# Float64 weights to float32 by bit shifts in a fused attention, mixture-of-experts and dense kernel

## Chip, cores and metric

The kernel runs on one core of one Trainium2 chip. The metric is the device time of one execution in microseconds. [...]

## The reference

```python
# attention, per head; q, k, v: (4, 12, 448, 64) float32
scores = cap * np.tanh(scale * np.matmul(q, k.transpose(0, 1, 3, 2)) / cap)
attn = softmax(scores); x = attn @ v            # -> (1792, 768)
# experts: 8 experts of 4 slots; w1 (8, 768, 1024), w2 (8, 1024, 768) float32
logits = x @ phi                                 # (1792, 32)
slot_input = softmax(logits, axis=0).T @ x
slot_out = relu(slot_input[e] @ w1[e]) @ w2[e]   # for each expert e
x = softmax(logits, axis=1) @ slot_out
# dense layer: w_in (768, 2048), w_out (2048, 768)
r = np.maximum(x @ w_in, 0.0)
return (s * (r * r) + b) @ w_out                 # (1792, 768) float32
```

The cap is 30. w_in and w_out reach the kernel as float64 (their scale factor is a double), 12.6 MB each; all other inputs are float32.

## The kernel before

The kernel writes its instruction order by hand: a planner (`ListSchedule`) gets each piece of work with an engine, a cost, its needs and its buffers, simulates the engines with these costs, and emits the pieces in the order in which they would start. Each engine then works through its own queue in that order and waits where a semaphore asks for it. There is one plan for attention and one for the dense layer; the stage between them is in plain program order.

Attention walks over 24 pairs of heads. TensorE makes scores (`sp`, L452), ScalarE takes tanh and exp (L459, L472), GpSimd sums exponentials over rows (`es`, L482 and L485), TensorE multiplies with v (`av`, L494), and VectorE copies and splits q, k and results (L355, L402, L578). For matmuls in the fast float32 format operands are split into a high and a low part.

w_in and w_out are cut into 32 tiles of 128 x 768 weights (even numbers from w_in, odd from w_out). `load_words` reads a tile of float64 as pairs of 32-bit words, low word first, 768 KB. The converter works in three functions: `conv_a` masks out the exponent as 16-bit numbers (`ce`, L206) and the top 20 bits of the mantissa with a leading one set (`cm`, L207) on VectorE; `conv_f` (L214) rebuilds the exponent on ScalarE; `conv_b` puts the sign in (L217) and adds the low word (L221) on VectorE; `conv_m` (L227) multiplies mantissa by power of two on GpSimd. The first 14 tiles are converted within attention (pieces `cl`, `ca`, `cf`, `cb`, `cmul`, `cst` of the first plan) and stored as float32 in DRAM (`scr`), to be loaded again later; when the last is stored, `cend` frees room and opens the further loads of expert weights. The other 18 tiles are converted inside the dense layer (`ld`, `ca`, `cf`, `cb`, `w`).

Between the two lie the slots and the experts: weights of 48.6 MB stream in through rings of buffers (`w1c`, `w2c`), the later ones in room that attention gives back.

The dense layer goes in 64 steps: four blocks of tokens (three of 512, one of 256) times 16 column groups f. A step makes h by one matmul (`gp`, L1091), squares and scales it on ScalarE (L1108, L1115, L1121 twice), takes the low part on VectorE (`gl`, L1136), and adds to the result by matmuls of L1159 and L1160 with the high and low parts of h and of w_out. For each f of the first block the weights must be ready: w_out is split into high (L1046, L1048) and low (L1051, GpSimd); w_in is multiplied with the slot outputs (`ma`, `ms`, `mb`, `mc`, `ml`, L1060 to L1084). Output leaves in L1168 to L1179.

At the very end a flag decides whether everything runs once more in a safe form (`run(True)`); before, the flag depends on the cap alone and the second run does not happen on these inputs.

Of the kernel before, what the change touches and what calls it, by code (L numbers as in the profile page):

```python
# [1 line left out]

# [6 lines left out]
F32 = mybir.dt.float32  # L9
F32R = mybir.dt.float32r  # L10
I32 = mybir.dt.int32
# [8 lines left out]

CAP_FAST = 32.0
EPS = 1e-9


ACT, DVE, POOL, PE, SP = "ACT", "DVE", "POOL", "PE", "SP"
# [66 lines left out]
def kernel(  # L92
# [54 lines left out]
    capsq = const.tile([1, 1], F32, name="capsq")  # L147
    nc.vector.tensor_tensor(out=capsq, in0=capt[0:1], in1=capt[0:1], op=ALU.mult)
    nc.vector.tensor_scalar(out=flag, in0=capsq, scalar1=CAP_FAST * CAP_FAST, scalar2=None, op0=ALU.is_gt)


    wide = w_in.dtype != F32
# [37 lines left out]
    def load_words(i, pool):  # L190
        kb, fn = (KDM, FC) if i % 2 == 0 else (1, DM)
        t = pool.tile([128, kb, fn * 2], I32, tag="w", name="w64")
        nc.sync.dma_start(out=t, in_=w_rows(i, 2))
        return t

    def conv_a(t, pool, bufs):
        nn = t.shape[1] * t.shape[2] // 2  # L200
        hi = t.rearrange("p k (f x) -> p (k f) x", x=2)[:, :, 1]
        top = t.rearrange("p k f -> p (k f)").bitcast(U16)
        top = top.rearrange("p (f x) -> p f x", x=4)[:, :, 3]
        e = pool.tile([128, nn], U16, tag="ce", name="ce", bufs=bufs[0])
        m = pool.tile([128, nn], I32, tag="cm", name="cm", bufs=bufs[1])
        nc.vector.tensor_scalar(out=e, in0=top, scalar1=0x7FF0, scalar2=None, op0=ALU.bitwise_and)  # L206
        nc.vector.tensor_scalar(  # L207
            out=m, in0=hi, scalar1=0x000FFFFF, scalar2=0x00100000,
            op0=ALU.bitwise_and, op1=ALU.bitwise_or,
        )  # L210
        return t, top, e, m

    def conv_f(t, top, e, m):
        nc.scalar.activation(out=e, in_=e, func=AF.Relu, scale=8.0, bias=ebias)  # L214

    def conv_b(t, top, e, m):
        nc.vector.scalar_tensor_tensor(  # L217
            out=e, in0=top, scalar=0x8000, in1=e, op0=ALU.bitwise_and, op1=ALU.bitwise_or
        )
        lo = t.rearrange("p k (f x) -> p (k f) x", x=2)[:, :, 0].bitcast(U32)  # L220
        nc.vector.scalar_tensor_tensor(  # L221
            out=m.bitcast(F32), in0=lo, scalar=2.0 ** -32, in1=m, op0=ALU.mult, op1=ALU.add
        )

    def conv_m(t, top, e, m):
        f = m.bitcast(F32)
        nc.gpsimd.tensor_tensor(out=f, in0=f, in1=e.bitcast(BF16), op=ALU.mult)  # L227
        return f


    def run(safe):
# [40 lines left out]
        def cv_f(i, _):  # L272
            conv_f(*env[i])

        def cv_b(i, _):
            conv_b(*env[i])

        def cv_m(i, _):
            env[i] = conv_m(*env[i])

        def cv_store(i, _):
            nc.sync.dma_start(out=scr[i], in_=env.pop(i))
# [399 lines left out]
        def op(name, engs, f, need=(), prio=0.0, acq=(), rel=(), **kw):  # L682
            sch.add(name, engs, lambda e: f(*name[1:], e), need, prio, acq, rel, **kw)
# [133 lines left out]
        for i in range(len(cvs)):  # L817
            pr = CV0 + CVP * i
            op(("cl", i), [(SP, 2.19)], cv_load, [], pr - 6, [("w", i)], lat=LAT, after=CVA)
            op(("ca", i), [(DVE, 0.94)], cv_a, [("cl", i)], pr, [("cm", i), ("ce", i)])  # L820
            op(("cf", i), [(ACT, 0.83)], cv_f, [("ca", i)], pr)
            op(("cb", i), [(DVE, 1.74)], cv_b, [("cf", i)], pr, [], [("w", i)])
            op(("cmul", i), [(POOL, 1.6)], cv_m, [("cb", i)], pr, [], [("ce", i)])
            op(("cst", i), [(SP, 1.1)], cv_store, [("cmul", i)], pr, [], [("cm", i)], lat=LAT)
            need = [("cst", j) for j in range(i + 1)]

# [181 lines left out]
        def gtile():  # L1008
            return ps_g.tile([128, 512], F32, tag="g", name="gp")
# [3 lines left out]
        raw, cva, wih, mst, msb, woh, wol, hg = {}, {}, {}, {}, {}, {}, {}, {}  # L1013

        def is_words(i):
            return wide and i >= 2 * XS

        def load_w(i, _):
            if is_words(i):
                raw[i] = load_words(i, st_p)  # L1020
                return
            raw[i] = cv_p.tile([128, NE1], F32, tag="cm", name="w32")
            if wide:
                nc.sync.dma_start(out=raw[i], in_=scr[i])
            else:
                nc.sync.dma_start(
                    out=raw[i].rearrange("p (k f) -> p k f", k=KDM if i % 2 == 0 else 1), in_=w_rows(i, 1)
                )

        def emit_ca(i, _):  # L1030
            cva[i] = conv_a(raw.pop(i), cv_p, (NCE, NCM))

        def emit_cf(i, _):
            conv_f(*cva[i])

        def emit_cb(i, _):
            conv_b(*cva[i])

        def emit_cm(i, _):
            raw[i] = conv_m(*cva.pop(i))  # L1040

        def emit_hi(f, e):
            t = wo_tile(f)
# [149 lines left out]
        def call(f, *a):  # L1193
            return lambda e: f(*a, e)

        sch.add("sot", [(DVE, 0.3)], call(emit_sot), after=3.2)
        for i in range(NI):
            f, rows = divmod(i, 2)
            pr = float(f)
            if is_words(i):  # L1200
                sch.add(("ld", i), [(SP, 2.19)], call(load_w, i), prio=pr - WL, acq=[("stg", i)], lat=2.0)
                sch.add(
                    ("ca", i), [(DVE, 0.94)], call(emit_ca, i), [("ld", i)], pr, [("cm", i), ("ce", i)]
                )
                sch.add(("cf", i), [(ACT, 0.83)], call(emit_cf, i), [("ca", i)], pr)
                sch.add(("cb", i), [(DVE, 1.74)], call(emit_cb, i), [("cf", i)], pr, rel=[("stg", i)])
                sch.add(("w", i), [(POOL, 1.6)], call(emit_cm, i), [("cb", i)], pr, rel=[("ce", i)])
            else:
                sch.add(("w", i), [(SP, 1.1)], call(load_w, i), prio=pr, acq=[("cm", i)], lat=2.0)
            if rows:  # L1210
                need = [("w", i)] + (["sot"] if f >= WE else [])
                sch.add(("hi", f), [(ACT, 0.73)] + [(DVE, 0.87)] * (f < FD), call(emit_hi, f), need, pr)
                sch.add(("lo", f), [(POOL, 1.76)], call(emit_lo, f), [("hi", f)], pr, rel=[("cm", i)])
            else:
                pm = pr - PM

                d = 0.45 if f > 2 else 0.9
                ga, gb = ("g", ("a", f)), ("g", ("b", f))
                sch.add(
                    ("ma", f), [(PE, d)], call(emit_ma, f), [("w", i), "sot"], pm, [ga], [("cm", i)]  # L1220
                )
                sch.add(("ms", f), [(ACT, 0.16)], call(emit_ms, f), [("ma", f)], pm, [("ms", f)], [ga])
                sch.add(("mb", f), [(PE, d / 2)], call(emit_mb, f), [("ms", f)], pm, [gb], [("ms", f)])
                sch.add(("mc", f), [(ACT, 0.16)], call(emit_mc, f), [("mb", f)], pm)
                sch.add(("ml", f), [(DVE, 0.2)], call(emit_ml, f), [("mc", f)], pm, rel=[gb])
        prev = ["sot"]
        for x, (t0, n, f) in enumerate(steps):
            ph = x - PH
# [67 lines left out]
```

## Time and profile before

| | us |
|---|---|
| median of 3 runs | 684.87 |
| lowest and highest run | 681.32, 689.25 |
| the profiled execution | 681.37 |
| its span, first to last instruction | 679.6 |
| VectorE busy | 423.9 (62%) |
| TensorE busy | 597.6 (88%) |
| ScalarE busy | 411.0 (60%) |
| GpSimd busy | 275.2 (40%) |

PE is TensorE's matmuls, PEld its weight loads, DVE VectorE, ACT ScalarE, POOL GpSimd, SP the queue that issues most DMAs. A busy share counts an instruction from its start to its end, also where it waits inside. A row by stage gives the stretch, its length, then busy us (with the number of instructions) of PE, PEld, DVE, ACT and POOL, then TensorE's granted clock as a share of full speed, the DMA share and GB/s. The stages by the timeline: attention up to 291 us, slots and experts up to 368.8, the dense layer after that, with its last matmul at 671.9.

### The profile page before, as it was taken

How to read it: one execution, taken by the hardware profiler on the slowest of the kernel's cores; microseconds unless marked ns; L12 is line 12 of the kernel's file. 1: busy time of each engine (PE TensorE's matmuls, PEld its weight loads, DVE VectorE, ACT ScalarE, POOL GpSimd, SP SyncE). 2: the span in 40 equal slices, each digit the busy share in tenths (PEclk: the TensorE clock that was granted, in tenths of full speed). 3: DMA queues.
4: the chain of work that ended last, by engine and by line, in shares of the span. 5: the costliest groups of instructions: out<-in, count | busy, mean ns of one | idle time of the engine just before them, and what ended most of it. 6: DMA issues, size and time to landing. Idle time of an engine off the chain costs nothing.

```text
span 679.6 us, 10379 instructions
## 1 busy us (share of the span) xinstructions
PE 597.6 (88%) x3992; PEld 410.8 (60%) x3992; DVE 423.9 (62%) x614; ACT 411.0 (60%) x572; POOL 275.2 (40%) x200
## 2 busy tenths in 40 slices
PE   6987979988898899889866968777999999999995
PEld 4554544554454445446524756555888888888884
DVE  5799998999999996455402799999411112111211
ACT  6978675767697587400004766546666667666693
POOL 1797579769778795200004455565300000000000
PEclk9999898989999999969967988878999999999999
DMA  6798878997658379889999734440020002000201
GB/s 168 199 297 260 255 221 265 291 249 203 178 165 225 104 222 304 324 327 404 406 417 400 253 117 136 145 158 26 18 76 1 1 1 93 1 1 1 93 1 51
DMA packets 58362, 119.94 MB, mean 176 GB/s; under 512 B 4864, under 2 KB 35072, under 8 KB 58304
## 3 DMA queue, kind: packets, MB, share of 16 engines
q1 hardware_dynamic: 57360, 119.09, 53.9%
q8 instruction: 33, 0.54, 0.3%
q10 hardware_dynamic: 944, 0.10, 0.1%
q14 instruction: 25, 0.20, 0.1%
HBM read 97.62 MB, written 11.01 MB: 160 GB/s over the span
## 4 chain that ended last, share of the span: by engine, by line
PE 49%; DVE 34%; DMA 9%; issue 5%; ACT 2%; POOL 1%; SPq 0%; DVEq 0%; ACTq 0%
PE y L1159 19%; PE y L1160 10%; DVE cm L221 5%; DMA w2c<-in_moe_w_dram 5%; DVE cm L207 5%; PE sp L452 4%; PE av L494 4%; DVE ce L206 3%; DVE ks L402 3%; DVE qs L402 3%; DVE ce L217 3%; DVE ks L355 2%; DVE qs L355 2%; PE h1p L915 2%; PE gp L1091 2%
## 5 line engine op out<-in xcount | busy, mean ns | idle before, releaser
L1136 DVE TENSOR_TENSOR gl<-r,gh 128x512 fp32r<-128x512 f32 (+1 forms) x65 | 47.4, 730 | 146.6 <-ACT r L1121 146.3
L1159 PE MATMUL y<-wo,gh 128*128 128x512 f32 x336 | 130.6, 410 | 0.0
L459 ACT ACTIVATE e<-sp,tsc 112x896 f32<-112x896 f32 x96 | 92.6, 1005 | 38.8 <-PE sp L452 32.4
L485 POOL TENSOR_TENSOR es<-es,e 112x448 f32<-112x448 f32 x92 | 111.0, 1217 | 6.6 <-ACT e L472 3.0
L1160 PE MATMUL y<-wo,gh 128*128 128x256 f32 x336 | 96.9, 289 | 0.0
L452 PE MATMUL sp<-qs,ks 128*112 128x448 f32 x384 | 95.6, 390 | 1.5 <-ACT e L459 1.4
L472 ACT ACTIVATE e<-e,capt 112x896 f32<-112x896 f32 x96 | 95.2, 1042 | 0.3
L494 PE MATMUL av<-e,vn 112*64 112x448 f32 x384 | 86.0, 569 | 4.1 <-ACT ce L214 3.1
L452 PEld LDWEIGHTS sp<-qs,ks 128*112 128x112 f32 x384 | 65.5, 182 | 32.4 <-ACT e L459 8.5
L482 POOL TENSOR_TENSOR es<-e 112x448 f32<-112x448 f32 x48 | 66.7, 1404 | 42.2 <-PE dn L513 35.3
L227 POOL TENSOR_TENSOR cm<-cm,ce 128x768 f32<-128x768 f32 x32 | 59.2, 1850 | 51.2 <-DVE cm L221 36.4
L1159 PEld LDWEIGHTS y<-wo,gh 128*128 128x128 f32 x336 | 65.6, 195 | 13.7 <-issue 2.0
L1108 ACT ACTIVATE r<-gp 128x512 f32<-128x512 f32 (+1 forms) x65 | 34.9, 538 | 58.2 <-PE gp L1091 56.9
L1159 PE MATMUL y<-wo,gl 128*128 128x512 f32 x168 | 68.1, 405 | 1.6 <-DVE gl L1136 1.6
L1160 PEld LDWEIGHTS y<-wo,gh 128*128 128x128 f32 x336 | 66.1, 197 | 1.7
L1121 ACT ACTIVATE gh<-r,bt,st 128x512 fp32r<-128x512 f32 (+1 forms) x65 | 49.1, 756 | 1.7
L1121 ACT ACTIVATE r<-r,bt,st 128x512 f32<-128x512 f32 (+1 forms) x65 | 49.1, 756 | 1.6
L494 PEld LDWEIGHTS av<-e,vn 112*64 112x64 f32 x384 | 24.7, 140 | 40.3 <-issue 30.6
L1160 PE MATMUL y<-wo,gl 128*128 128x256 f32 x168 | 48.5, 289 | 0.0
L214 ACT ACTIVATE ce<-ce,ebias 128x768 uint16<-128x768 uint16 x32 | 29.7, 935 | 29.8 <-DVE ce L206 29.8
L221 DVE SCALAR_TENSOR_TENSOR cm<-w,cm 128x768 f32<-128x768 uint32 x32 | 47.2, 1475 | 0.0
L1159 PE MATMUL y<-woe,gh 128*128 128x512 f32 x112 | 44.3, 416 | 0.0
(143 smaller groups left out, 983.6 us busy)
## 6 DMA issues: line engine op xcount, KB each, us to landing
w1c<-in_moe_w_dram SPq DMA_DIRECT2D x24, 1024.0 KB, 9.0
w2c<-in_moe_w_dram SPq DMA_DIRECT2D x26, 768.0 KB, 13.7
w<-in_moe_w_in_dram SPq DMA_DIRECT2D x16, 768.0 KB, 5.3
w<-in_moe_w_out_dram SPq DMA_DIRECT2D x16, 768.0 KB, 4.6
qs<-qs SPq DMA_DIRECT2D x23, 448.0 KB, 4.7
qn<-in_q_dram SPq DMA_DIRECT2D x24, 224.0 KB, 4.1
kn<-in_k_dram SPq DMA_DIRECT2D x24, 224.0 KB, 4.5
vn<-in_v_dram SPq DMA_DIRECT2D x24, 224.0 KB, 5.0
```

What stands on the lines that cost most here:

```text
L221: nc.vector.scalar_tensor_tensor(out=m.bitcast(F32), in0=lo, scalar=2.0 ** -32, in1=m, op0=ALU.mult, op1=ALU.add)
L227: nc.gpsimd.tensor_tensor(out=f, in0=f, in1=e.bitcast(BF16), op=ALU.mult)
L452: nc.tensor.matmul(out=sp[:, cc, 0:S], lhsT=ks[n][:, h, r * P:(r + 1) * P], rhs=qs[n][:, h, i, :], start=(i == 0), stop=(i == 1),)
L459: nc.scalar.activation(out=e, in_=spt.pop((u, h))[:, :, 0:S], func=AF.Tanh, scale=tsc[0:P])
L472: nc.scalar.activation(out=e, in_=e, func=AF.Exp, scale=capt[0:P])
L482: eng.tensor_tensor(out=t, in0=x[:, 0], in1=x[:, 1], op=ALU.add)
L485: eng.tensor_tensor(out=t, in0=t, in1=x[:, cc], op=ALU.add)
L494: nc.tensor.matmul(out=avt[n][64 * h:64 * h + 64, 0:S], lhsT=vt[n][:, h, r, :], rhs=et[u, h][:, cc], start=(r == 0), stop=(r == R - 1),)
L1121: nc.scalar.activation(out=out, in_=in_, func=AF.Identity, scale=st, bias=bt)
L1136: eng.tensor_tensor(out=gl, in0=t, in1=f32(gh), op=ALU.subtract)
L1159: nc.tensor.matmul(out=ya, lhsT=lhsT, rhs=w[:, 0:512], start=first, stop=last)
L1160: nc.tensor.matmul(out=yb, lhsT=lhsT, rhs=w[:, 512:768], start=False, stop=last and i0 == per - 1)
```

## The change

A float32 pattern is now built in integers: the high word shifted left by three and masked, with sign and top exponent bit put back (two VectorE instructions, `conv_a`), plus the low word times 2^-29 (made by ScalarE in `conv_f`), added as an integer (`conv_m`): by GpSimd in attention, by VectorE in the dense layer. This holds only for weights in float32's normal range, so from step 15 of the dense layer on all 32 tiles are loaded a second time and their least and greatest high word is taken (`note_range`); the closing test (`flag_range`) sets the flag of the safe run. The old converter stays under the names `any_a`, `any_f` and `any_m` for that run, which now converts all tiles anew. Costs and buffer releases in the two plans change with it. Since the first two functions no longer share a buffer in one direction, `conv_f` needs the load only; the plans still put it behind `conv_a`.

The diff, without the imports and unchanged surroundings:

```diff
     capsq = const.tile([1, 1], F32, name="capsq")
     nc.vector.tensor_tensor(out=capsq, in0=capt[0:1], in1=capt[0:1], op=ALU.mult)
     nc.vector.tensor_scalar(out=flag, in0=capsq, scalar1=CAP_FAST * CAP_FAST, scalar2=None, op0=ALU.is_gt)
+    big_cap = const.tile([1, 1], F32, name="big_cap")
+    nc.vector.tensor_copy(out=big_cap, in_=flag)
+    onec = const.tile([128, 1], F32, name="onec")
+    nc.vector.memset(onec, 1.0)
...
     def conv_a(t, pool, bufs):
+        nn = t.shape[1] * t.shape[2] // 2
+        hi = t.rearrange("p k (f x) -> p (k f) x", x=2)[:, :, 1]
+        c = pool.tile([128, nn], I32, tag="ce", name="ce", bufs=bufs[0])
+        m = pool.tile([128, nn], I32, tag="cm", name="cm", bufs=bufs[1])
+        nc.vector.tensor_scalar(
+            out=m, in0=hi, scalar1=3, scalar2=0x3FFFFFF8, op0=ALU.logical_shift_left, op1=ALU.bitwise_and
+        )
+        nc.vector.scalar_tensor_tensor(
+            out=m, in0=hi, scalar=-0x40000000, in1=m, op0=ALU.bitwise_and, op1=ALU.bitwise_or
+        )
+        return t, c, m
+
+    def conv_f(t, c, m):
+        lo = t.rearrange("p k (f x) -> p (k f) x", x=2)[:, :, 0].bitcast(U32)
+        nc.scalar.activation(out=c, in_=lo, func=AF.Copy, scale=2.0 ** -29)
+
+    def conv_m(t, c, m, e):
+        (nc.gpsimd if e == POOL else nc.vector).tensor_tensor(out=m, in0=m, in1=c, op=ALU.add)
+        return m.bitcast(F32)
+
+
+
+
+    def any_a(t, pool, bufs):
         nn = t.shape[1] * t.shape[2] // 2
         hi = t.rearrange("p k (f x) -> p (k f) x", x=2)[:, :, 1]
...
-    def conv_f(t, top, e, m):
+    def any_f(t, top, e, m):
         nc.scalar.activation(out=e, in_=e, func=AF.Relu, scale=8.0, bias=ebias)
 
-    def conv_b(t, top, e, m):
+    def any_m(t, top, e, m):
         nc.vector.scalar_tensor_tensor(
             out=e, in0=top, scalar=0x8000, in1=e, op0=ALU.bitwise_and, op1=ALU.bitwise_or
...
-
-    def conv_m(t, top, e, m):
         f = m.bitcast(F32)
         nc.gpsimd.tensor_tensor(out=f, in0=f, in1=e.bitcast(BF16), op=ALU.mult)
         return f
+
+
+    rng = const.tile([128, 2, NI], F32, name="rng")
+
+    def note_range(i, t):
+        hi = t.rearrange("p k (f x) -> p (k f) x", x=2)[:, :, 1].bitcast(F32)
+        for j, o in enumerate((ALU.min, ALU.max)):
+            nc.vector.tensor_reduce(
+                out=rng[:, j, i:i + 1], in_=hi, axis=AX.X, op=o, apply_absolute_value=True
+            )
+
+    def flag_range(ps):
+
+        ends = const.tile([128, 2], F32, name="ends")
+        off = const.tile([128, 2], F32, name="off")
+        for j, (o, lim, out_of) in enumerate(((ALU.min, LEAST, ALU.is_lt), (ALU.max, MOST, ALU.is_ge))):
+            nc.vector.tensor_reduce(out=ends[:, j:j + 1], in_=rng[:, j, :], axis=AX.X, op=o)
+            nc.vector.tensor_scalar(out=off[:, j:j + 1], in0=ends[:, j:j + 1], scalar1=lim, scalar2=None, op0=out_of)
+        nc.tensor.matmul(out=ps[0:1, 0:2], lhsT=onec, rhs=off, start=True, stop=True)
+        tot = const.tile([1, 1], F32, name="tot")
+        nc.vector.tensor_reduce(out=tot, in_=ps[0:1, 0:2], axis=AX.X, op=ALU.add)
+        nc.vector.tensor_tensor(out=tot, in0=tot, in1=big_cap, op=ALU.add)
+        nc.vector.tensor_scalar(out=flag, in0=tot, scalar1=0.0, scalar2=None, op0=ALU.is_gt)
 
 
...
-        def cv_b(i, _):
-            conv_b(*env[i])
-
-        def cv_m(i, _):
-            env[i] = conv_m(*env[i])
+        def cv_m(i, e):
+            env[i] = conv_m(*env[i], e)
...
             op(("cl", i), [(SP, 2.19)], cv_load, [], pr - 6, [("w", i)], lat=LAT, after=CVA)
-            op(("ca", i), [(DVE, 0.94)], cv_a, [("cl", i)], pr, [("cm", i), ("ce", i)])
-            op(("cf", i), [(ACT, 0.83)], cv_f, [("ca", i)], pr)
-            op(("cb", i), [(DVE, 1.74)], cv_b, [("cf", i)], pr, [], [("w", i)])
-            op(("cmul", i), [(POOL, 1.6)], cv_m, [("cb", i)], pr, [], [("ce", i)])
+            op(("ca", i), [(DVE, 1.6)], cv_a, [("cl", i)], pr, [("cm", i), ("ce", i)], [("w", i)])
+            op(("cf", i), [(ACT, 0.83)], cv_f, [("ca", i)], pr, [], [("w", i)])
+            op(("cmul", i), [(POOL, 1.75)], cv_m, [("cf", i)], pr, [], [("ce", i)])
             op(("cst", i), [(SP, 1.1)], cv_store, [("cmul", i)], pr, [], [("cm", i)], lat=LAT)
...
         def is_words(i):
-            return wide and i >= 2 * XS
+            return wide and (safe or i >= 2 * XS)
...
-            if wide:
+            if wide and not safe:
                 nc.sync.dma_start(out=raw[i], in_=scr[i])
...
         def emit_ca(i, _):
-            cva[i] = conv_a(raw.pop(i), cv_p, (NCE, NCM))
+            cva[i] = (any_a if safe else conv_a)(raw.pop(i), cv_p, (NCE, NCM))
 
         def emit_cf(i, _):
-            conv_f(*cva[i])
-
-        def emit_cb(i, _):
-            conv_b(*cva[i])
-
-        def emit_cm(i, _):
-            raw[i] = conv_m(*cva.pop(i))
+            (any_f if safe else conv_f)(*cva[i])
+
+        def emit_cm(i, e):
+            raw[i] = any_m(*cva.pop(i)) if safe else conv_m(*cva.pop(i), e)
+
+
+        def emit_rl(i, _):
+            raw["r", i] = load_words(i, st_p)
+
+        def emit_rr(i, _):
+            note_range(i, raw.pop(("r", i)))
+
+        def emit_rf(_):
+            flag_range(gtile())
...
@@ -1200,17 +1258,19 @@
             if is_words(i):
                 sch.add(("ld", i), [(SP, 2.19)], call(load_w, i), prio=pr - WL, acq=[("stg", i)], lat=2.0)
                 sch.add(
-                    ("ca", i), [(DVE, 0.94)], call(emit_ca, i), [("ld", i)], pr, [("cm", i), ("ce", i)]
-                )
-                sch.add(("cf", i), [(ACT, 0.83)], call(emit_cf, i), [("ca", i)], pr)
-                sch.add(("cb", i), [(DVE, 1.74)], call(emit_cb, i), [("cf", i)], pr, rel=[("stg", i)])
-                sch.add(("w", i), [(POOL, 1.6)], call(emit_cm, i), [("cb", i)], pr, rel=[("ce", i)])
+                    ("ca", i), [(DVE, 1.6)], call(emit_ca, i), [("ld", i)], pr, [("cm", i), ("ce", i)],
+                    [("stg", i)],
+                )
+                sch.add(("cf", i), [(ACT, 0.83)], call(emit_cf, i), [("ca", i)], pr, rel=[("stg", i)])
+                sch.add(
+                    ("w", i), [(POOL if safe else DVE, 0.9)], call(emit_cm, i), [("cf", i)], pr, rel=[("ce", i)]
+                )
             else:
                 sch.add(("w", i), [(SP, 1.1)], call(load_w, i), prio=pr, acq=[("cm", i)], lat=2.0)
             if rows:
                 need = [("w", i)] + (["sot"] if f >= WE else [])
                 sch.add(("hi", f), [(ACT, 0.73)] + [(DVE, 0.87)] * (f < FD), call(emit_hi, f), need, pr)
-                sch.add(("lo", f), [(POOL, 1.76)], call(emit_lo, f), [("hi", f)], pr, rel=[("cm", i)])
+                sch.add(("lo", f), [(POOL, 1.9)], call(emit_lo, f), [("hi", f)], pr, rel=[("cm", i)])
...
+        if wide and not safe:
+            for i in range(NI):
+                pr = MC + 2 + i
+                need = [("y", MC - 1 + i // 2, 0)]
+                sch.add(("rl", i), [(SP, 2.19)], call(emit_rl, i), need, pr - WL, [("stg", ("r", i))], lat=10.0)
+                sch.add(("rr", i), [(DVE, 1.9)], call(emit_rr, i), [("rl", i)], pr, rel=[("stg", ("r", i))])
+            sch.add(
+                "rf", [(PE, 0.1)], call(emit_rf), [("rr", i) for i in range(NI)], MC + 2 + NI,
+                [("g", "rf")], [("g", "rf")], lat=1.0,
+            )
```

## Rows read from the trace of the kernel before

**Rows 1.** Chain that ended last, shares of the span by engine (whole span)

```profile
PE 49%; DVE 34%; DMA 9%; issue 5%; ACT 2%; POOL 1%; SPq 0%; DVEq 0%; ACTq 0%
```

**Rows 2.** Busy time by stage (columns: section on the profile)

```profile
34.00:242.00 208.00, 183.35 (x1011) 101.16 (x1010) 200.80 (x295) 148.00 (x164) 163.15 (x123) 0.96 0.78 226
...
291.00:368.80 77.80, 60.69 (x986) 34.17 (x986) 27.57 (x59) 5.27 (x14) 4.50 (x4) 0.85 0.99 390
...
374.00:476.00 102.00, 81.28 (x491) 62.43 (x490) 97.90 (x97) 62.03 (x105) 57.17 (x28) 0.87 0.41 138
476.00:671.90 195.90, 195.11 (x1098) 169.65 (x1095) 40.78 (x59) 131.56 (x207) 5.36 (x3) 0.99 0.07 25
```

**Rows 3.** Busy time, 255 to 272 us, same columns

```profile
255.00:272.00 17.00, 17.00 (x102) 8.87 (x100) 11.22 (x21) 12.88 (x15) 9.69 (x10) 1.00 0.92 308
```

**Rows 4.** Groups by line, VectorE, 0 to 290: count, busy us, mean ns

```profile
L221 DVE SCALAR_TENSOR_TENSOR cm<-w,cm 128x768 f32<-128x768 uint32 x14 | 20.5, 1464 | 0.0
L217 DVE SCALAR_TENSOR_TENSOR ce<-w,ce 128x768 uint16<-128x768 uint16 x14 | 17.0, 1213 | 0.0
L206 DVE TENSOR_SCALAR ce<-w 128x768 uint16<-128x768 uint16 x14 | 16.7, 1196 | 2.3 <-DMA w<-in_moe_w_in_dram 2.3
...
L207 DVE TENSOR_SCALAR cm<-w 128x768 int32<-128x768 int32 x14 | 16.3, 1162 | 0.0
```

**Rows 5.** Single lines, whole span: least, median, greatest duration in ns

```profile
L206 DVE TENSOR_SCALAR ce<-w x32: 541/558/3108, 32.1 to 466.9; 128x768 uint16<-128x768 uint16 x32
L207 DVE TENSOR_SCALAR cm<-w x32: 542/1480/2200, 32.6 to 467.4; 128x768 int32<-128x768 int32 x32
L217 DVE SCALAR_TENSOR_TENSOR ce<-w,ce x32: 894/959/2955, 39.7 to 473.4; 128x768 uint16<-128x768 uint16 x32
L221 DVE SCALAR_TENSOR_TENSOR cm<-w,cm x32: 944/956/2603, 40.7 to 475.7; 128x768 f32<-128x768 uint32 x32
L227 POOL TENSOR_TENSOR cm<-cm,ce x32: 1634/1664/3160, 42.6 to 478.4; 128x768 f32<-128x768 f32 x32
L1051 POOL TENSOR_TENSOR woe<-w,woe x4: 1808/1816/1819, 364.3 to 371.2; 128x768 fp32r<-128x768 f32 x4
```

**Rows 6.** Timeline, 402.3 to 402.7: start us, duration us, instruction

```profile
402.38 1.83 POOL L227 TENSOR_TENSOR cm<-cm,ce 128x768 f32<-128x768 f32 x1 [2.29 <-issue]
402.64 1.99 DVE L207 TENSOR_SCALAR cm<-w 128x768 int32<-128x768 int32 x1
```

**Rows 7.** Groups by line, 374 to 476: gl on VectorE, and GpSimd

```profile
L1136 DVE TENSOR_TENSOR gl<-r,gh 128x512 fp32r<-128x512 f32 x13 | 15.5, 1190 | 1.9 <-ACT r L1121 1.9
L227 POOL TENSOR_TENSOR cm<-cm,ce 128x768 f32<-128x768 f32 x17 | 33.4, 1967 | 42.9 <-DVE cm L221 28.2 <-issue 11.0 <-PE y L1160 3.8
L1051 POOL TENSOR_TENSOR wo<-cm,wo 128x768 fp32r<-128x768 f32 x8 | 19.2, 2395 | 0.9 <-ACT wo L1046 0.9
L1051 POOL TENSOR_TENSOR wo<-w,wo 128x768 fp32r<-128x768 f32 x3 | 6.4, 2143 | 1.9 <-ACT wo L1046 1.9
```

**Rows 8.** Chain that ended last, in order of time, 285 to 375: its longest piece

```profile
322.21 16.61 DMA w2c<-in_moe_w_dram
```

**Rows 9.** Timeline of a steady dense step, 520 to 526

```profile
520.33 0.39 PE L1091 MATMUL gp<-cs,mst 128*128 128x512 f32 x1
...
523.75 0.69 DVE L1136 TENSOR_TENSOR gl<-r,gh 128x512 fp32r<-128x512 f32 x1 [3.70 <-ACT r L1121]
...
524.72 0.39 PE L1091 MATMUL gp<-cs,mst 128*128 128x512 f32 x1
...
525.65 0.39 PE L1159 MATMUL y<-wo,gl 128*128 128x512 f32 x1
```

**Rows 10.** Groups by line, whole span: VectorE reductions in SBUF

```profile
L561 DVE TENSOR_REDUCE lr<-lw 112x128 f32<-112x512 f32 x8 | 8.4, 1054 | 0.2
...
L951 DVE TENSOR_REDUCE cmx<-lall 112x16 f32<-112x512 f32 x1 | 0.6, 644 | 0.0
```

More of the change, by code (lines that the diff above doesn't have):

```diff
@@ L1 @@
 from contextlib import ExitStack
+import numpy as np
 import concourse.bass as bass
@@ L22 @@
 EPS = 1e-9
+LEAST, MOST = (float(np.array(x, np.uint32).view(np.float32)) for x in (0x38100000, 0x47F00000))
 ACT, DVE, POOL, PE, SP = "ACT", "DVE", "POOL", "PE", "SP"
```

## The prediction

> **What bounds the kernel now.** I read four views: the chain of work that ended last, then engine busy times by stage, then the groups of instructions by line inside a stage, then the timeline where a group's mean lay far above its minimum.
>
> The chain gives TensorE 49% and VectorE 34% of the span [rows 1], but a share over the whole span mixes stages. Split by stage [rows 2], four pictures appear. In attention (34 to 242 us), while weights are being converted, VectorE is busy 200.8 of 208 us and TensorE 183.4. From 291 to 368.8 (slots and experts) the DMA share is 0.99 and nothing else is full. From 374 to 476 (dense layer, the last 18 conversions) VectorE is busy 97.9 of 102 us, TensorE 81.3 at a granted clock of 0.87. From 476 on TensorE has 195.1 of 195.9 us and VectorE only 40.8. So VectorE decides in the two stages where the converter runs, and only there. The counter-sample is 255 to 272, attention with its conversions done: VectorE falls to 11.2 of 17 us and TensorE has no gap at all [rows 3].
>
> Next, why the converter is dear. Its four VectorE instructions cost 20.5 + 17.0 + 16.7 + 16.3 = 70.5 us for 14 tiles in attention [rows 4], 5.04 us a tile. Their minima are 0.54, 0.54, 0.89 and 0.94 us, 2.92 together [rows 5]. The rest is waiting inside the instruction: the mask of L207 starts at 402.64, 0.26 us after GpSimd began an L227, and ends at 404.63, 0.42 us after that L227 did [rows 6]. An L207 met like this takes 1.99 us instead of 0.54. So whatever takes instructions of this sort off VectorE saves their waits too, and whatever takes work off GpSimd shortens the others.
>
> **The change part by part.**
> *Attention, 14 tiles.* Out go four VectorE instructions; in come two, a shift-and-mask (form of L207) and a mask-and-or with two SBUF inputs (form of L217 and L221). I price them at attention's means, 1.16 and (1.46 + 1.21)/2 = 1.34 us [rows 4]: 2.50 a tile, 35.0 for 14, so 35.5 us of VectorE time go. With the minima 0.54 + 0.94 it would be 49.7, with the dearest means 1.20 + 1.46 still 33. The ScalarE pass is replaced by one over as many elements, behind the load alone; at worst a few tenths more on an engine busy 148.0 of 208 [rows 2]. GpSimd's float multiply becomes an integer add of the same size: no integer operation stands in the trace, so between 1.63 us (minimum of L227 [rows 5]) and 1.97 (its mean in the dense layer [rows 7]); I take no change. GpSimd there is at 163.2 of 208.
>
> What comes late next is TensorE. Its 183.4 busy us cap the gain at 208 - 183.4 = 24.6 us, so 35.5 us of VectorE do not become 35.5 us of time. How much does? At 66% VectorE the gap in TensorE was 0 [rows 3], at 97% it was 12%. With about 33 us off, VectorE stands at 168 of some 196 us, 86%; a straight line between the two samples gives a gap of 7% and a gain of 10 us. Queues grow faster than a straight line close to full, so I take 13, with 0 and 24.6 as bounds.
>
> *Slots and experts.* Nothing in them changes. The chain there is weight loads (16.6 us for one stretch [rows 8]) fed by buffers that attention frees, and by a gate that opens when the last converted tile is stored. Both move earlier with the conversions, so the stage moves as a block and keeps the 13 us.
>
> *Dense layer, 18 tiles.* VectorE has three instructions for four, the new one the integer add that GpSimd loses (two SBUF inputs, so L221's 0.94 as least [rows 5], its mean in attention, 1.46, at most [rows 4]). GpSimd keeps only L1051. Because the two engines hold each other up, I add them. Before, at minima: VectorE 18 x 2.92 = 52.6 and 13 of gl at 0.69 = 9.0 [rows 7, 9]; GpSimd 17 x 1.634 = 27.8 and 11 x 1.808 = 19.9 [rows 5, 7]. Together 109.3 for a stretch of 102, a factor of 0.933. After: VectorE 18 x (0.54 + 0.94 + 0.94) = 43.6 and 9.0, GpSimd 19.9: 72.5, times 0.933 is 67.6 us. TensorE comes up again: 81.3 x 0.87 = 70.7 us at full clock, ScalarE 62.0 [rows 2]. With three engines between 62 and 71 I take 75 us, a gain of 27. Best 71 (gain 31); worst, the waits stay in sum as they are and only one instruction's shortest time goes, 18 x 0.54, a gain of 10.
>
> The Trainium skill is stricter (SBUF — State Buffer, Who interferes with whom): the port pair that VectorE and GpSimd share is held for a whole instruction by a GpSimd one or by a VectorE one with two SBUF inputs, and the other side stands still. By it the add moved to VectorE speaks against the change wherever L1051 runs, and the factor would be 1 and the stretch 72.5 us instead of 67.6; the rows, with 109.3 us of work in 102, show some overlap, and either figure lies under the 75 taken.
>
> *Range test.* 32 more loads of 768 KB and 64 reductions over 768 elements, from step 15 of the dense layer on, two tiles a step. The loads run where the DMA share is 0.07 [rows 2]; without that cover they would add 25 MB to the stage at 0.99. Their price on SP is queue places among output stores, whose buffers are not wanted again for 16 steps. A reduction reads every second word; L221 reads the same stride at 0.94 us for 768, and L951 takes 0.64 for 512 in one pass [rows 5, 10]. So 0.95 each, 1.90 a tile; two tiles and one gl are 2 x 1.90 + 0.69 = 4.49 us against a step of 4.39 (520.33 to 524.72 [rows 9]). gl ends at 524.44 and its first reader starts at 525.65, 1.2 us of slack; a tile's two reductions ahead of it take up to 0.7 more. With 16 such steps the bounds are 0 and 11 us; the excess of 0.1 a step and one pause for the closing matmul, which waits on VectorE, make it 3.
>
> A rule against this part: the Trainium skill (Vector Engine (DVE) Microarchitecture Reference, Measured stream behaviour on trn2) lets a port run at full rate only on pairs of adjacent words, and gives up to 1.73 ns an element where one source hops singly. By it a reduction would be about 1.33 us (an estimate) and the range test near 26 us dearer. The row of L221, single words at every second place and 0.94 us, speaks against applying it here.
>
> **Sum.** 13 + 27 - 3 = 37 us off the profiled execution's 681.37 (span 679.6 and 1.8 around it): 644.4. The median of the runs is 684.87, 3.5 above that execution; I forecast for such a median: 648.
>
> **Rivals.**
> *Attention keeps its length.* The planner orders all of attention anew from its costs, and its order can put TensorE behind other latencies; only the dense layer gains: 648 + 13 = 661. For it: a cap only 24.6 away; against it: [rows 3].
> *Both stages reach TensorE's bound* and the range test hides: 24.6 + 31 = 55.6 off, 629.
> *The dense layer stays tied to VectorE*, waits as long as today: gain 10 instead of 27, 665.
> *Slow reductions.* L561 reduces 512 strided elements in 1.05 us [rows 10], twice L951. If the stride is the cause and not its 128 short groups, 768 take 1.59, a tile 3.18, a step 2 x 3.18 + 0.69 = 7.05 for 4.39, over 16 steps 43 instead of 3: 688, no change. The stream rule named above points the same way.
> *Slower: GpSimd adds integers slowly.* Place: its queue in 34 to 242, where 13 adds at today's 1.70 are part of its 163.2 us. GpSimd without them needs 141; the dense layer's 24 net are used up when the stretch is 232 long, that is from 7.0 us an add. At 8 us the stretch is 245 and the time 698. Against it: every row of GpSimd, though of floats, runs near 2.1 ns an element.
>
> **Chances.** Forecast 60 in 100 (its own range 638 to 656), attention keeps its length 14, both bounds 8, dense tied 6, slow reductions 6, slow adds 6. From 629 to 666 holds the first four, less the far tail of the third and part of the spread of the others, about 84 in 100. A difference of about 1% is what a measurement can tell here: faster by more 0.88, within it 0.06 (slow reductions), slower 0.06 (slow adds).
>
> **What the changed profile would show.** Right: the shift and the mask-or near 1.2 and 1.3 us in attention; VectorE under 90% in the converting part of attention, TensorE above 93%; experts starting some 13 us sooner; the last conversion some 75 us after the first of the dense layer; range reductions at 0.95 us; dense steps of about 4.4 to 4.6 us while they run. Wrong: VectorE still full in attention; reductions at 1.5 us or more with gaps in TensorE before gl's readers; integer adds over 3 us; or weight loads that start no sooner.

## The result and the profile after

| | before | after |
|---|---|---|
| median of the runs, us | 683.1 (4 runs) | 662.07 (4 runs, 658.46 to 665.38) |
| ratio | | 0.9678, 95% interval 0.9592 to 0.9765 |
| profiled execution, its span, us | 681.37, 679.6 | 661.14, 659.3 |

The median of before, 683.1, counts one run more (680.57 us) than the 684.87 shown ahead. The change takes 3.2%: faster, and inside the forecast range, but 14 us above the forecast of 648. The profiled pair lies 20.2 us apart. Split at the first matmul of the experts (`h1p`) and at the first matmul (`gp`) of dense steps 0, 16 and 63:

| stretch, us | before | after | difference | forecast |
|---|---|---|---|---|
| start to first `h1p` (attention, slots) | 296.0 | 295.3 | -0.7 | -13 |
| to step 0 (experts) | 69.6 | 71.3 | +1.7 | 0 |
| steps 0 to 16 (conversions) | 118.3 | 92.5 | -25.8 | -27 |
| steps 16 to 63 | 182.5 | 185.1 | +2.6 | +3 |
| step 63 to the end | 13.1 | 15.1 | +2.0 | 0 |

One term failed, attention. Its stage rows of after answer to [rows 2, 3] (same columns; the dense layer cut at its own bounds):

```profile
34.00:242.00 208.00, 182.41 (x1016) 102.21 (x1016) 172.82 (x276) 148.42 (x165) 153.94 (x124) 0.96 0.93 248
255.00:272.00 17.00, 17.00 (x97) 9.58 (x97) 10.23 (x18) 14.47 (x16) 10.11 (x9) 1.00 0.53 179
...
366.00:459.00 93.00, 85.66 (x570) 68.05 (x565) 74.77 (x88) 73.53 (x130) 32.45 (x16) 0.93 0.58 195
459.00:657.00 198.00, 190.07 (x1060) 162.82 (x1058) 93.57 (x127) 127.33 (x200) 0.00 (x0) 0.99 0.46 152
```

In 34 to 242 VectorE fell from 200.8 to 172.8 us, as wanted, and TensorE did not rise: 183.4 before, 182.4 now. What rose is the DMA share, from 0.78 to 0.93. Cut finer, the stretch shows where, first before:

```profile
34.00:187.00 153.00, 135.09 (x752) 74.52 (x751) 147.04 (x219) 108.20 (x121) 118.86 (x91) 0.96 0.84 246
187.00:242.00 55.00, 48.27 (x261) 26.64 (x259) 53.76 (x77) 39.80 (x44) 44.28 (x32) 0.97 0.60 168
```

Then after:

```profile
34.00:187.00 153.00, 128.11 (x702) 72.10 (x703) 129.36 (x203) 105.60 (x119) 116.13 (x92) 0.95 0.99 260
187.00:242.00 55.00, 54.30 (x316) 30.11 (x314) 43.46 (x73) 42.82 (x47) 37.81 (x33) 0.99 0.77 214
```

In its first 153 us the DMA share is 0.99 (before 0.84, at VectorE 147.0 of 153), and TensorE has 128.1 us where it had 135.1. The bytes moved rose far less than the share, from 246 to 260 GB/s. From 187 on, with transfers at 0.77, TensorE is full: 54.3 of 55. So a part of attention got slower and a part got faster. The chain of waits names what was late. By engine over the whole span, answering to [rows 1], and then its pieces in order of time (start, length, what) around the longest wait; another, of 9.28 us, lies at 149.54:

```profile
PE 57%; DMA 18%; DVE 17%; issue 4%; ACT 1%; SPq 1%; ACTq 0%; DVEq 0%
```

```profile
170.69 0.64 DVE qs L454
171.32 0.02 issue
171.34 13.50 DMA qs<-qs
184.84 0.04 issue
184.89 3.24 PE sp L504 x8
```

`qs<-qs` (L457) copies a split q tile of 448 KB from one half of the partitions to the other; the scores of the next pair of heads wait for it. It is not a load from memory, but it goes through the same queue and the same DMA engines as the loads. Its rows of the waits in after (total us, times, longest us), and the line on its landing:

```profile
PE sp L504 <- DMA qs<-qs: 15.7, 7, 3.5
...
PEld sp L504 <- DMA qs<-qs: 5.0, 2, 2.7
```

```profile
DMA to landing us min/median/max: 3.8/6.4/13.5
```

Before:

```profile
DMA to landing us min/median/max: 3.8/4.7/9.6
```

The views of before show no wait of TensorE for it; after it waits 15.7 + 5.0 = 20.7 us. The converter, faster by two VectorE passes, asks for its 768 KB tiles sooner: the last converted tile of attention is stored at 203.5 us instead of 244.6. The copy, which has a deadline, now shares the DMA engines with that crowd. After 203.5 the transfers run dry: 0.53 from 255 to 272, where before had 0.92 [rows 3].

The new instructions themselves cost about what the prediction said, or less (durations in ns: least, median, greatest; answers to [rows 5]):

```profile
L214 DVE TENSOR_SCALAR cm<-w x32: 498/557/3312, 34.1 to 444.1; 128x768 int32<-128x768 int32 x32
L217 DVE SCALAR_TENSOR_TENSOR cm<-w,cm x32: 957/959/3580, 34.9 to 444.7; 128x768 int32<-128x768 int32 x32
L227 DVE CUSTOM_DVE_ANT_0 cm<-cm,ce x18: 946/959/2630, 383.1 to 448.1; 128x1536 uint16<-128x1536 uint16 x18
L227 POOL TENSOR_TENSOR cm<-cm,ce x14: 1805/1830/1862, 46.3 to 201.6; 128x768 int32<-128x768 int32 x14
L268 DVE TENSOR_REDUCE rng<-w x64: 942/946/952, 472.5 to 575.2; 128x1 f32<-128x768 f32 x64
```

### The profile page after: what moved, and what is told of

Its sections match the earlier page's. It is cut to its first block, busy times and chain, and to the rows that moved or that the text cites. A ratio compares the mean times of both kernels' runs of the same rounds, so it can differ in the third digit from the quotient of the medians.

```text
span 659.3 us, 10415 instructions
## 1 busy us (share of the span) xinstructions
PE 588.4 (89%) x3994; PEld 405.7 (62%) x3994; DVE 417.5 (63%) x643; ACT 409.4 (62%) x570; POOL 227.1 (34%) x182
## 3 DMA queue, kind: packets, MB, share of 16 engines
q1 hardware_dynamic: 72208, 144.26, 70.6%
## 4 chain that ended last, share of the span: by engine, by line
PE 57%; DMA 18%; DVE 17%; issue 4%; ACT 1%; SPq 1%; ACTq 0%; DVEq 0%
PE y L1217 21%; PE y L1218 10%; DMA qs<-qs 8%; PE sp L504 8%; PE av L546 5%; DMA w2c<-in_moe_w_dram 5%; DVE cm L214 3%; PE h1p L966 2%; DVE cm L227 2%; PE gp L1149 2%; DVE qs L454 2%; DVE qs L407 2%; DVE ks L407 2%; DVE cm L217 2%; DMA w<-scr 1%
## 5 line engine op out<-in xcount | busy, mean ns | idle before, releaser
L1217 PE MATMUL y<-wo,gh 128*128 128x512 f32 x336 | 127.6, 402 | 0.0
L537 POOL TENSOR_TENSOR es<-es,e 112x448 f32<-112x448 f32 x92 | 104.9, 1150 | 25.5 <-ACT e L524 21.7
L504 PE MATMUL sp<-qs,ks 128*112 128x448 f32 x384 | 96.9, 394 | 16.3 <-DMA qs<-qs 15.7
L1194 DVE TENSOR_TENSOR gl<-r,gh 128x512 fp32r<-128x512 f32 (+1 forms) x65 | 41.5, 639 | 95.5 <-ACT r L1179 95.4
L1218 PE MATMUL y<-wo,gh 128*128 128x256 f32 x336 | 94.7, 282 | 0.0
L534 POOL TENSOR_TENSOR es<-e 112x448 f32<-112x448 f32 x48 | 60.7, 1280 | 40.7 <-PE dn L565 23.0
L1217 PEld LDWEIGHTS y<-wo,gh 128*128 128x128 f32 x336 | 63.5, 189 | 13.8 <-issue 1.6
L1218 PEld LDWEIGHTS y<-wo,gh 128*128 128x128 f32 x336 | 63.4, 189 | 1.7
L268 DVE TENSOR_REDUCE rng<-w 128x1 f32<-128x768 f32 x64 | 57.0, 946 | 0.0
L1104 ACT CAST woe<-w 128x768 fp32r<-128x768 f32 x3 | 2.5, 834 | 66.5 <-DMA w<-scr 66.5
L217 DVE SCALAR_TENSOR_TENSOR cm<-w,cm 128x768 int32<-128x768 int32 x32 | 40.7, 1272 | 1.1
```

Source lines behind the costliest of these rows:

```text
L217: nc.vector.scalar_tensor_tensor(out=m, in0=hi, scalar=-0x40000000, in1=m, op0=ALU.bitwise_and, op1=ALU.bitwise_or)
L268: nc.vector.tensor_reduce(out=rng[:, j, i:i + 1], in_=hi, axis=AX.X, op=o, apply_absolute_value=True)
L504: nc.tensor.matmul(out=sp[:, cc, 0:S], lhsT=ks[n][:, h, r * P:(r + 1) * P], rhs=qs[n][:, h, i, :], start=(i == 0), stop=(i == 1),)
L534: eng.tensor_tensor(out=t, in0=x[:, 0], in1=x[:, 1], op=ALU.add)
L537: eng.tensor_tensor(out=t, in0=t, in1=x[:, cc], op=ALU.add)
L1194: eng.tensor_tensor(out=gl, in0=t, in1=f32(gh), op=ALU.subtract)
```

## Experiments

Two explanations of the unchanged attention stood against each other. *Crowding*: the freed VectorE time went into waits for transfers that the faster converter crowds together. *Order or TensorE* (the named rival): the new plan order, or TensorE itself, holds attention whatever the transfers do.

**Loads left out.** In both kernels only the first two float64 tiles of attention are loaded and used again for the other twelve; everything else runs as it was.

```diff
+        held = {}
...
-            env[i] = load_words(i, c_p)
+            if i < 2:
+                held[i] = load_words(i, c_p)
+            env[i] = held[i % 2]
```

> The changed kernel, with 12 of the 14 float64 loads of attention left out: tiles 2 to 13 are made from the words of tiles 0 and 1, so the output is not the reference's. Every engine's work, its order and the stores to DRAM stay; 9.4 MB less go over the DMA queue in attention. Crowding (the DMA share of 0.99 between 34 and 187 us makes the copy qs<-qs of q land late and TensorE waits for it): the copies land in under 5.5 us at the median instead of 6.4, TensorE waits under 8 us for them instead of 20.7, and the experts' first matmul (h1p) comes at 280 to 288 us instead of 295.3. Order (the new plan's order of TensorE and VectorE costs as much as the converter saves): h1p at 293 or later. Floor (TensorE cannot do attention faster): the same, 293 or later, with TensorE busy over 95% from 34 to 187.

Measured: 650.51 us in one execution; experts from 287.2, q copies landing in 4.6 us at the median, TensorE's wait for them 2.6 us instead of 20.7.

```profile
34.00:187.00 153.00, 138.52 (x777) 76.69 (x777) 143.47 (x216) 113.91 (x128) 123.24 (x97) 0.96 0.74 214
```

> The kernel before, with the same 12 loads left out (output not the reference's). Crowding as an effect of the change alone: before, VectorE set the pace and the DMA did not, so h1p stays at 291 to 297 us (296.0 before) and the time within 5 us of the kernel before. If the DMA was a bound already before: h1p at 288 or earlier, as much sooner as in the changed kernel.

Measured: 684.45; experts from 298.1 (with its loads 296.0).

```profile
34.00:242.00 208.00, 182.42 (x1004) 100.44 (x1004) 202.25 (x295) 146.00 (x162) 159.33 (x120) 0.96 0.62 179
```

The kernel before gains nothing although its DMA share falls to 0.62: VectorE still has 202 of 208 us. So attention before was held by VectorE, as the prediction read it, and after seems held by transfers. Both are single executions, and the next run shows how far one may be trusted.

**Without the range test.** The loop that plans the second loads, the reductions and the flag is left out, and with them that part of the computation.

```diff
-        if wide and not safe:
+        if False:
             for i in range(NI):
                 pr = MC + 2 + i
```

> The changed kernel without the range test: no second loads, no reductions, no closing matmul; the flag depends on the cap alone. If the range test costs what the blocks after the first lost, the steps of the later blocks go back from 4.46 to 4.39 us and the time falls by 2 to 4 us (0.3 to 0.6%). If the reductions are hidden and something else makes the steps 4.46, they stay at 4.46 and the time stays within 1 us, apart from the end after the last matmul (9.5 us, 7.7 before).

Measured: 662.02 us, ratio 0.9667 (0.9594 to 0.9739): no measurable difference to after. The profiled execution of it took only 651.7, with experts from 287.3, although its attention is that of after instruction for instruction. Its q copies landed in 5.3 us at the median and held TensorE for 6.1 us. So attention varies by 8 us or more from one execution to the next, and a single one can't decide about a gain of this size; the 287.2 without the loads is no earlier than this 287.3 with all of them.

```profile
34.00:187.00 153.00, 135.83 (x775) 75.77 (x776) 145.39 (x215) 113.70 (x128) 122.52 (x96) 0.98 0.97 273
```

The same executions say something on the order. In three profiled executions of after (two of them from the runs further down), in the kernel with loads left out and in this one, every engine has the same instructions of attention in the same order. Their experts start at 295.3, 299.0, 299.3, 287.2 and 287.3 us, and TensorE waits 20.7, 19.2, 11.9, 2.6 and 6.1 us for q copies. So the order alone doesn't hold attention at 295. From the scores of the 7th pair of heads to those of the 16th, after falls 9.9 us further behind this execution; the nine q copies in between took 84.2 us to land, added up, and here 62.3.

In the dense layer it is steadier: steps 16 to 63 take 184.2 us, 0.9 less than with the test, and 1.7 more than before.

**The old converter in attention, the new one in the dense layer.** The conversion steps of attention and their costs in the plan are put back (`cv_b` holds L217 and L221 of before); the instruction order on TensorE is then that of before.

```diff
-            env[i] = conv_a(env[i], c_p, (2, 3))
+            env[i] = any_a(env[i], c_p, (2, 3))
...
-            conv_f(*env[i])
+            any_f(*env[i])
+        def cv_b(i, _):
...
-            op(("ca", i), [(DVE, 1.6)], cv_a, [("cl", i)], pr, [("cm", i), ("ce", i)], [("w", i)])
...
+            op(("ca", i), [(DVE, 0.94)], cv_a, [("cl", i)], pr, [("cm", i), ("ce", i)])
...
+            op(("cb", i), [(DVE, 1.74)], cv_b, [("cf", i)], pr, [], [("w", i)])
```

> The dense layer's part of the change alone, with the range test: attention has the old converter with its old costs in the plan. If attention's part gave nothing, the time is that of the changed kernel within 4 us (658 to 666) and h1p comes near 296. If attention's part gave a gain that something later takes back, this run is slower than the changed kernel by 8 us or more; if it did harm, faster by 5 or more.

> The changed kernel, unaltered, as the yardstick for the three runs beside it on the same chip, and to see how much its attention differs between executions: without the range test the same attention had h1p at 287.3 us in one execution, 295.3 here. Crowding: time 655 to 667, spread over its executions over 5 us, h1p between 287 and 299, later when the q copies land later.

> The dense layer's part alone once more, now beside the changed kernel. What attention's part of the change is worth is this time less that of the changed kernel. Prediction on record: 13 us. Crowding: 0 to 8 us, because the DMA gives part of it back.

Measured: first 667.18, ratio 0.9713 (0.9654 to 0.9771). Then, in five rounds on one chip, after 664.28, 0.9673 (0.9629 to 0.9718), and the old attention 665.79, 0.9705 (0.9669 to 0.9740). The two intervals overlap: the attention half of the change, 0.3% or 1.5 us by the medians, can't be told from nothing. The first of these times lies 1 us above what was expected if attention's part gave nothing. In the profiled executions the experts start at 304.5 and 300.0 us with the old attention and at 299.0 in after beside them, so the 296.0 of before may be early for the old converter: it comes from one of the fastest executions of before. The rest of it alone gives nearly the whole gain, 685.61 to 667.18 on the first chip.

**The copies on another queue.** The q copies are issued by ScalarE, so that they need not stand behind loads in SP's queue; their entry in the plan moves with them.

```diff
-            nc.sync.dma_start(out=f32(qs[n][64:128]), in_=f32(qs[n][0:64]))
+            nc.scalar.dma_start(out=f32(qs[n][64:128]), in_=f32(qs[n][0:64]))
...
-                op(dup[0], [(SP, 1.27)], emit_dup, [("lo", "q", n, j) for j in range(2)], f + PD, lat=LAT)
+                op(dup[0], [(ACT, 0.3)], emit_dup, [("lo", "q", n, j) for j in range(2)], f + PD, lat=LAT)
```

> The changed kernel with the q copies issued from ScalarE's queue instead of SP's, so they don't stand behind the weight loads in one queue; the bytes are the same. If the copies are late because they queue behind other transfers: they land in under 5 us at the median, and h1p comes 4 to 10 us sooner, less what ScalarE loses on 23 issues. If the 16 DMA engines themselves are full, whatever the queue: landing stays at 6 us or more and the time within 2 us, or slower, since ScalarE waits in order for q's low part.

Measured: 665.22, ratio 0.9703 (0.9658 to 0.9748), experts from 296.9. No gain. The copies took 7.0 us to land at the median, 6.8 in after beside it, so the place in SP's queue isn't what makes the landing slow. TensorE's wait for them fell from 19.2 to 9.5 us all the same and the experts began 2.1 us sooner, in one execution of each; the time did not follow.

**The loads spaced.** In the plan a float64 load of attention may not start before a time of its own, 14 or 11 us (by the plan's clock) after the one ahead; in the third kernel below the loads of expert weights in attention are spaced too.

```diff
-            op(("cl", i), [(SP, 2.19)], cv_load, [], pr - 6, [("w", i)], lat=LAT, after=CVA)
+            op(("cl", i), [(SP, 2.19)], cv_load, [], pr - 6, [("w", i)], lat=LAT, after=CVA + 11.0 * i)
...
-                prev + [("cend",)] * (i >= first), 1e3 + i, after=WA,
+                prev + [("cend",)] * (i >= first), 1e3 + i, after=WA + 11.0 * min(i, first) * (not safe),
```

> The changed kernel with one size changed: in the plan of attention the load of float64 tile i may start 14 i us after the first instead of as soon as a buffer is free, so the same 14 loads spread over the whole of attention. Crowding: DMA share in 34 to 187 under 0.93 instead of 0.99, q copies land in under 5.7 us at the median, TensorE's waits for them fall from 20.7 to under 10 us, h1p 4 to 10 us sooner than in the changed kernel beside it, time 3 to 10 us less. Order or floor: no difference, or slower by what the later end of the conversions costs the expert weights.

> As with a pace of 14, but 11 i us: the plan now ends the conversions at 184.9 us of its own time, where the kernel before had 191.1 and the changed kernel has 154.8. Pace 14 made attention 7 us shorter and the experts' stage 15 us longer, since the gate for the later expert weights opened late. Crowding: with pace 11 the gate opens near 240 us, early enough; the copies land in under 6 us at the median, h1p 3 to 7 us before that of the changed kernel beside it, the experts no longer than its 54, and the time 2 to 7 us less. If the DMA up to the end of the experts is one full resource, then what attention gains the experts lose, and the time stays within 2 us.

> Pace 11 for the float64 loads, and the first 12 loads of expert weights spread in the same way (load i not before 30.4 + 11 i us of the plan). Crowding: DMA share in 34 to 187 falls below 0.90, TensorE's waits for q copies below 8 us, h1p 4 to 9 us sooner than in the changed kernel beside it and the time 3 to 9 us less. If the DMA up to the end of the experts is one full resource: no gain, or a loss, since less is loaded when attention ends.

> The changed kernel again, as the yardstick on this chip: 655 to 668 us, h1p 287 to 300, copies landing in 6 to 7 us at the median, first block of the dense layer 91 to 95 us.

Measured, 14 us apart: 672.37, ratio 0.9782 (0.9741 to 0.9823). Experts start at 292.0 (299.0 in after on this chip), but the dense layer at 378.2: the last conversion is stored at 272.6, the further expert weights wait for that gate, and the experts take some 15 us longer, so that the time lies 8 us above after. 11 us apart: 660.64, 0.9611 (0.9570 to 0.9652), against 0.9641 (0.9606 to 0.9676) for after on the same chip, not to be told apart. TensorE's wait for q copies fell to 5.0 us, but from 120 to 160 us, into which five loads of expert weights fall, the DMA share was still 1.03, and VectorE waited 15.4 us for float64 tiles (8.3 in after). So the q copies are not the whole price of the crowd; how it divides among the copies and the other transfers stays open. With both kinds of load spaced: 650.72, ratio 0.9489 (0.9443 to 0.9536), 10 us below after on the same chip, and below both kernels. In this kernel TensorE waits 0.2 us for q copies; their landing, and the stage:

```profile
DMA to landing us min/median/max: 3.9/4.4/7.9
```

```profile
34.00:187.00 153.00, 141.08 (x801) 77.86 (x802) 137.17 (x216) 115.20 (x129) 122.86 (x97) 0.98 0.89 257
34.00:242.00 208.00, 192.60 (x1103) 105.29 (x1104) 186.30 (x298) 157.39 (x176) 168.00 (x133) 0.98 0.86 249
```

TensorE has 192.6 of 208 us, and its experts start at 282.2 against 296.0 before: 13.8 us by one execution of each, and about the 13 that the prediction gave to attention. The GB/s of its first row are nearly those of after, 257 against 260, at a DMA share of 0.89 against 0.99.

**The spacing with the old converter.** The last edit, made on the kernel with the old attention converter.

> The changed kernel with the old converter inside attention (as in e4_att_old and e6_att_old_again), and the float64 loads and expert-weight loads of attention spaced 11 apart in the plan, as in e10_pace11_w11. It asks whether the 10 us that the spacing brought need the new converter. Theory (two limits in attention, VectorE with the old converter, crowded transfers with the new one, so that both have to go): with the old converter VectorE stays over 90% busy in 34 to 242 us, experts begin near 297 to 303 us as in the unspaced old form, ratio 0.966 to 0.974 (663 to 668 us), while q copies land in under 5 us. Rival (the spacing is worth its 10 us whatever the converter; the new converter in attention is worth nothing): experts begin near 285 us, ratio 0.950 to 0.958 (651 to 657 us). In between, 0.958 to 0.966: each brings a part by itself.

Measured: 665.30, ratio 0.9664 (0.9625 to 0.9703), experts from 297.9; q copies land in 4.0 us and cost TensorE 1.2.

```profile
34.00:242.00 208.00, 185.69 (x1016) 103.53 (x1016) 197.04 (x299) 149.97 (x165) 154.11 (x122) 0.95 0.80 225
```

The four cases together (ratios; each by the before on its own chip, and not all on one chip):

| attention | loads as they were | loads spaced |
|---|---|---|
| old converter | 0.9713, 0.9705 | 0.9664 |
| new converter | 0.9678, 0.9673, 0.9641 | 0.9489 |

With the old converter VectorE is nearly full (197 of 208) and the spacing brings 0.4 to 0.5%, with overlapping intervals; without the spacing the new converter brings 0.3% on the same chip, also overlapping. With the new converter the spacing brings 1.5% on the same chip, and with the spacing the new converter brings 1.75%, 12 us, by ratios from two chips; both have separate intervals. The reading that fits all four: two limits lay close behind each other, and each hides what is gained at the other. Spacing also gives the planner another order on all engines, so the last cell may not be the crowd alone, and no run separates the two; but the plan with the old converter got the same spacing, and gained almost nothing.

## Why the prediction was right and wrong

**What bounded the kernel before**: right. VectorE held the two converting stages. Leaving loads out of attention changed nothing there, and the dense layer with its new converter gained alone nearly what the whole change did (0.9713 and 0.9705).

**Attention, 13 us**: the failed step is "What comes late next is TensorE". The prices under it were good: 0.81 us and 1.44 us for the two instructions in attention against 1.16 and 1.34 taken, so 31.5 us for 14 tiles against 35.0, and 28 us of VectorE's time gone from 34 to 242 against 33. But TensorE, which was to rise above 93%, has 182.4 of 208 us, 88%: it waited 20.7 us for a copy that the prediction doesn't have. The queue behind VectorE was chosen by busy shares of engines, and the DMA share of the same row [rows 2], 0.78 over the stage, was passed over. It was 0.84 in the first 153 us, and a converter that stops waiting for VectorE asks for the same bytes in less time: 0.99, with 6% more bytes in the stretch. So a sum of bytes alone would not have given 0.99. The transfers it crowded were not those that the change speaks of but a copy that the scores wait for. The straight line through [rows 3] hid this, since that sample, TensorE full at a DMA share of 0.92, seemed to say that transfers do no harm; in those 17 us a single q copy was issued, and it landed in 3.9 us.

**The rival "attention keeps its length"** gave 661, which is what came, with the chance of 14; the forecast range holds 662 because this rival was counted in. Its cause was not the one told: in the very order of after the experts began at 287.2 and 287.3 us in two other kernels, so the plan's order alone isn't what holds them. That the transfers are at fault rests above all on the spacing: with the new converter it gained 1.5% clear of noise, and with the old one next to nothing. Leaving the loads out points the same way, but weakly, being one execution. How much of the gain is the new order that comes with the spacing stays open.

**Experts move as a block**: they did, by the 0.7 us that there was to move. Their own 1.7 us stay open: three executions of after took 70.6 to 71.8, the two kernels with the plans of before 69.6 and 70.1. And the block holds only while the gate opens in time: with loads 14 us apart the experts took 86.2.

**Dense layer, 27 us**: the mechanism was right, and 25.8 is near, in part by luck. From the first conversion to the end of the last it took 71.4 us (377.7 to 449.1), between the best case of 71 and the 75 taken, where before it took 103.4 (377.0 to 480.4): 32.0 less. From there to step 16 TensorE, without a gap, needed 10.0 us and before 3.5, which gives 6.5 back. In 366 to 459 VectorE has 74.8 of 93 us, TensorE 85.7. The add on VectorE has a mean of 1.23 us, between the bounds 0.94 and 1.46. GpSimd adds 128x768 integers in 1.83 us, between 1.63 and 1.97, and the rival of slow adds falls. VectorE and GpSimd still hold each other up at times: L217 takes up to 2.64 us in this stretch, with 0.96 at the median, and all nine converter instructions of VectorE over 1 us started while GpSimd ran its subtraction for w_out (L1109, L1051 before).

**The rule on the shared port pair** (the Trainium skill, SBUF — State Buffer, Who interferes with whom) gave 72.5 us for that stretch and the sum by overlap 67.6: it took 71.4, nearer to the rule. The rows don't show that the port pair set this length, though: VectorE is busy 67.4 us of it and TensorE 64.6.

**Range test, 3 us**: the size was right, 2.6, and its parts not. The reductions take 0.946 us against 0.95, with the loads at a DMA share of 0.46 in cover, and no pause comes of them: from 480 to 600 us TensorE is busy 120.00 of 120.00. The growth is in the matmuls themselves. The wide one's median in the steady steps (480 to 556 us) went from 390 ns to 397, which over some ten of them in a step is the 0.07 us between the steps of 4.39 and 4.46 us. Without the range test it was 394 and the step 4.44. So 3 of the 7 ns go with the test, and what lengthens the matmuls stays open; no run here tried it. The rival of slow reductions falls with 0.946 us, and with it the adjacent-pair rule at this stride (the Trainium skill, Vector Engine (DVE) Microarchitecture Reference, Measured stream behaviour on trn2), by which one would take about 1.33 (an estimate).

**The tail**, 2.0 us longer, is no term of the prediction, and its cause stays open: three executions of after had 15.1 to 15.9 us, but other kernels with the range test from 13.2 to 15.6.

**Slips in the working**, without weight in the sum: L561's 1.05 us is 1.6 times L951's 0.64 and not twice, and GpSimd's rows run from 2.1 to 3.1 ns an element (1634 to 2395 ns for 768), not all near 2.1.

## What to carry to other kernels

When work is taken off the engine that decides, ask what else shares its pace: a producer that runs faster asks for its loads in less time, and a DMA share of 0.84 leaves little for that. The share can rise more than the bytes (here 0.84 to 0.99 for 6% more), so a sum of bytes is only a lower estimate of it; look in that stage for a small copy with a deadline. If such a copy is late, try spreading every bulk load that shares its time, not just those that changed: here only that was clear of noise. And a stage with two close limits may show nothing for removing either alone; test them as a square of four kernels.

## What the runs showed of the hardware

An integer add of two 128x768 int32 tiles on VectorE stands in the trace as a custom operation over 128x1536 16-bit halves and takes 0.96 us at the median, as much as a mask-and-or over 768 words (0.959). In after a copy inside SBUF of 448 KB took from 3.8 to 13.5 us to land. The DMA share alone doesn't settle it: at 0.97 one execution had copies of 5.3 us at the median, at 0.99 another had 6.4, and attention was 8 us longer.
